# A scan over chunks and a routed expert layer: first decays spread batch by batch, the inverse in two pieces, loads of x in halves

## The chip, the cores and the metric

The kernel runs on one core of a Trainium2 chip. The metric is the device time of one execution in microseconds (us), as the median of several runs. One execution was also taken by the hardware profiler. The engines are TensorE (PE; PEld is its weight load), VectorE (DVE), ScalarE (ACT), GpSimd (POOL) and SyncE (SP), which here issues nearly all loads.

## What is computed

Two parts follow each other. The first is a state-space scan over 768 positions for 4 batches and 8 heads, with head size D = 32 and state size N = 16. The second routes each of the 3072 resulting rows of 256 values to one of 8 experts by cosine similarity, and applies that expert's two matrices.

```python
log_a = np.log(np.clip(a, 1e-06, 1.0))
for c in range(S // 32):                       # the scan, chunk by chunk
    cum = np.cumsum(la, axis=-1)
    L = np.exp(cum[:, :, :, None] - cum[:, :, None, :]) * causal
    M = np.einsum('bhin,bhjn->bhij', Cc, Bc) * L
    y = np.einsum('bhij,bhjd->bhid', M, xc) \
      + np.einsum('bhin,bhnd->bhid', Cc, state) * np.exp(cum)[..., None]
    state = decay_full * state + sum_j(Bc_j xc_j * decay_from_j)
...
xn = x / (norm(x) + 1e-06);  en = expert_emb / (norm(expert_emb) + 1e-06)
logits = xn @ en.T / tau;  e = argmax(logits);  gate = softmax(logits)[e]
out[rows of e] = gate * (np.maximum(x @ w1[e], 0.0) @ w2[e])
```

## The kernel before

The scan goes over six chunks of Q = 128 positions. Each chunk is cut into two pairs of batches, so that there are twelve pairs p = 0..11 and twelve steps s. The order of work is written out by hand: every engine takes its instructions in the order in which the code writes them, and waits on semaphores only where data need it.

Decays are split into factors. `decays` (VectorE) turns the decays `a` of four chunks into running products `f` with one row per chunk, batch and head. `spread_decays` (TensorE, 16 matmuls, batch by batch and within it chunk by chunk) copies each row of `f` to all states of its head, in PSUM tiles `py` (chunks 0 and 1) and `pz` (chunks 2 and 3). `inverse` takes 1/f on VectorE into `r`, `turn_inverse` transposes it on TensorE, and ScalarE copies the outcome to `rT`. `keep_decays` (ScalarE) copies the spread decays of chunks 2 and 3 into `fr`.

For a chunk, `scale_c` makes `cp` = C times the spread decay, and `scale_x` makes `xs` = x times the inverse decay (128x1024, read from `in_x` and `rT`, both in SBUF). For a pair, `scores` multiplies B (`bz`) with `cp` into PSUM tiles `pgA` and `pgB`. `masks` keeps the causal half: VectorE multiplies `pgA` with a mask, while ScalarE copies `pgB` to `g` and GpSimd zeroes the upper half there (`affine_select`, named select below). `outputs` multiplies `g` with `xs` into `py`, `sums` multiplies B (`in_t`) with `xs` for the state, `tokens` turns the pair's outcome into rows.

`bz` has four places of 128x2x512, for chunks modulo 4. Chunks 0 and 1 are filled by ScalarE (`split_b`: two activations of 128x512 with a mask for each half of the states). Chunks 2 and 3, and later 4 and 5 in the places of 0 and 1, come by `load_two` (8 DMAs of 64 KB into the nonzero parts; the rest is cleared ahead by `clear_b` on ScalarE). SP issues the loads in the order of the code, and its DMAs use eight semaphores in turn: the ninth waits until the first has landed.

The start is `begin_scan`: loads, constants, decays, then pairs 0 and 1 up to their masks. `mamba` runs the steps from s = 1. There `outputs(p = s-1)`, at odd steps `sums`, and `tokens(p = s-2)` follow `scores(s)` and `masks(s)`. `norm_embeddings` squares the expert embeddings on ScalarE (`emb_sq`) and takes the root on GpSimd (`emb_r`). `place_consts` writes constants of the router on GpSimd. `fill` are matmuls on zeros that nobody reads. After the scan comes `moe`, 8 experts one after another.

## Time and profile before

| | |
|---|---|
| median of 3 runs | 239.04 us (238.05 to 240.39) |
| the profiled execution: its own time | 239.56 us |
| its span, first to last instruction | 237.8 us |
| TensorE busy, share of the span | 224.9 us, 95% |
| VectorE | 176.8 us, 74% |
| ScalarE | 129.7 us, 55% |
| GpSimd | 99.6 us, 42% |
| moved by DMA | 34.83 MB, mean 146 GB/s |

The scan takes the first 62 us, the experts the rest. Times in the rows below are us from the start of the span. A row of the timeline gives start, duration, engine, line and operation, output tile and input tiles, shape, the count of merged instructions, and in brackets how long the engine was idle before it and who ended that.

### The profile page before, as it was taken

The numbers are of one execution on the slowest core, as the hardware profiler recorded it, in microseconds if no ns is written. First come the engines' busy times: TensorE is split into PE (matmuls) and PEld (weight loads), VectorE is DVE, ScalarE is ACT, GpSimd is POOL, SyncE is SP. The second block draws the span as 40 slices with busy tenths as digits, with TensorE's granted clock in tenths as the row PEclk, the third lists the DMA queues.
The fourth block names the chain that finished last, engine by engine and source line by source line (L and its number), as shares of the span: only waits on it lengthen the run. The fifth ranks groups of instructions, "written<-read, shape, count | busy, mean of one in ns | idle before, by whom it ended". The sixth has DMA issues, their size and how long they took to land. (4 is left out here: it accounts for less than half of the span.)

```text
span 237.8 us, 6603 instructions
## 1 busy us (share of the span) xinstructions
PE 224.9 (95%) x2500; PEld 211.4 (89%) x2500; DVE 176.8 (74%) x467; ACT 129.7 (55%) x349; POOL 99.6 (42%) x125
## 2 busy tenths in 40 slices
PE   7899999999997999999999999999999999999980
PEld 7787878787896999999999999999999999999970
DVE  6896868897775727797768788877887978874850
ACT  6867666663540545652684467358446446637620
POOL 7835321173047507536417234631841623305113
PEclk9999999999999999999999999999999999999997
DMA  5878586475707932626245233824627444201001
GB/s 172 287 215 259 185 231 214 133 211 186 218 3 246 311 121 68 188 76 203 63 158 179 96 132 114 237 61 167 202 68 216 129 140 142 98 3 61 0 3 64
DMA packets 20978, 34.83 MB, mean 146 GB/s; under 512 B 2474, under 2 KB 13968, under 8 KB 20944
## 3 DMA queue, kind: packets, MB, share of 16 engines
q1 hardware_dynamic: 18256, 27.97, 37.5%
q0 software_dynamic: 2592, 6.39, 8.8%
q8 instruction: 20, 0.33, 0.6%
q14 instruction: 14, 0.11, 0.1%
q10 hardware_dynamic: 96, 0.03, 0.1%
HBM read 28.02 MB, written 6.42 MB: 145 GB/s over the span
## 5 line engine op out<-in xcount | busy, mean ns | idle before, releaser
L1141 POOL DMA_INDIRECT out_dram<-yo,to x26 | 29.3, 1128 | 61.5 <-ACT yo L1140 47.3
L1064 DVE TENSOR_TENSOR hT<-bank,hp 128x416 f32<-128x416 f32 (+6 forms) x42 | 22.0, 552 | 14.8 <-ACT hp L1058 9.7
L914 POOL DMA_INDIRECT xg<-rows,table x24 | 27.4, 1143 | 6.7 <-issue 4.5
L1058 ACT COPY hp<-bank 128x416 f32<-128x416 f32 (+6 forms) x42 | 19.9, 475 | 17.7 <-PE bank L1045 17.3
L1070 ACT ACTIVATE hT<-hT 128x416 f32<-128x416 f32 (+6 forms) x42 | 21.6, 524 | 11.3 <-DVE hT L1064 11.2
L628 POOL TENSOR_SCALAR_AFFINE_SELECT g<-g 128x1024 f32<-128x1024 f32 x13 | 17.0, 1315 | 25.6 <-ACT g L627 25.6
L1006 DVE TENSOR_TENSOR ws<-w 128x512 f32<-128x512 f32 x42 | 27.6, 683 | 0.0
L929 POOL TENSOR_TENSOR gr<-gr,half 128x3 f32<-128x3 f32 (+2 forms) x9 | 9.6, 1066 | 31.5 <-ACT sq L925 22.3
L1045 PE MATMUL bank<-ts,w 128*128 128x208 f32 (+6 forms) x112 | 21.8, 328 | 0.0
L1106 PE MATMUL bank<-ts,w 128*128 128x208 f32 (+6 forms) x112 | 21.4, 334 | 0.3 <-ACT yp L1119 0.3
L1045 PE MATMUL bank<-xT,w 128*128 128x208 f32 (+6 forms) x112 | 21.6, 326 | 0.0
L1045 PE MATMUL bank<-ts,ws 128*128 128x208 f32 (+6 forms) x112 | 20.6, 326 | 0.0
L1106 PE MATMUL bank<-hT,w 128*128 128x208 f32 (+6 forms) x112 | 19.5, 326 | 0.0
L1106 PE MATMUL bank<-ts,ws 128*128 128x208 f32 (+6 forms) x112 | 19.5, 326 | 0.0
L1106 PEld LDWEIGHTS bank<-ts,w 128*128 128x128 f32 x112 | 18.1, 190 | 1.3 <-ACT yp L1119 0.6
L1045 PEld LDWEIGHTS bank<-xT,w 128*128 128x128 f32 x112 | 18.8, 190 | 0.0
L1010 DVE TENSOR_TENSOR ts<-hT 128x416 f32<-128x416 f32 (+6 forms) x28 | 15.0, 556 | 5.1 <-ACT hT L1070 4.1
L1045 PEld LDWEIGHTS bank<-ts,ws 128*128 128x128 f32 x112 | 18.5, 190 | 0.1
L1045 PEld LDWEIGHTS bank<-ts,w 128*128 128x128 f32 x112 | 18.0, 190 | 0.5 <-ACT hp L1058 0.4
L1106 PEld LDWEIGHTS bank<-ts,ws 128*128 128x128 f32 x112 | 18.4, 190 | 0.0
L1106 PEld LDWEIGHTS bank<-hT,w 128*128 128x128 f32 x112 | 18.4, 190 | 0.0
L656 PE MATMUL py<-g,xs 128*32 128x128 f32 x384 | 14.1, 276 | 1.5 <-issue 1.1
(255 smaller groups left out, 499.1 us busy)
## 6 DMA issues: line engine op xcount, KB each, us to landing
w<-in_moe_w_dram SPq DMA_DIRECT2D x28, 512.0 KB, 4.3
rows<-yt SPq DMA_DIRECT2D x12, 264.0 KB, 2.3
in_x<-in_x_dram SPq DMA_DIRECT2D x6, 512.0 KB, 4.9
w<-in_moe_w_dram SPq DMA_DIRECT2D x8, 256.0 KB, 3.6
in_c<-in_CT_dram SPq DMA_DIRECT2D x6, 256.0 KB, 3.5
in_t<-in_B_dram SPq DMA_DIRECT2D x6, 256.0 KB, 3.4
bz<-in_BT_dram SPq DMA_DIRECT2D x16, 64.0 KB, 4.3
in_b<-in_BT_dram SPq DMA_DIRECT2D x2, 256.0 KB, 3.3
```

The costliest lines, as they stand in the source:

```text
L628: nc.gpsimd.affine_select(out=g, in_=g, pattern=[[0, 8], [1, Q]], compare_op=ALU.is_ge, fill=0.0, base=0, channel_multiplier=-1)
L656: nc.tensor.matmul(k.py[g : g + 32, v, 128 * i : 128 * i + 128], lhsT=t.xs[:, b + i, 4 * v + q, :], rhs=s.g[:, q, 2 * i + v, :], start=(c ...
L914: s.k.nc.gpsimd.indirect_dma_start(out=s.x[0:p, i, 0:TOK], out_offset=None, in_=rows, in_offset=bass.IndirectOffsetOnAxis(ap=s.at[0:p, i : ...
L929: nc.gpsimd.tensor_tensor(out=s.r[:], in0=s.r[:], in1=k.half[:, 0:nt], op=ALU.pow)
L1006: s.k.nc.vector.tensor_tensor(out=o, in0=in0, in1=in1, op=op)
L1010: s.k.nc.vector.tensor_tensor(out=t[i], in0=in0, in1=in1, op=ALU.subtract)
L1045: k.nc.tensor.matmul(out[:, g], lhsT=lhsT[:, f : f + 128], rhs=rhs, start=(g == 0 and i in (1, 2, 5)), stop=True, skip_group_check=True,)
L1058: nc.scalar.copy(out=u.p[:, {1: 0, 6: 1, 7: 2}[i]], in_=u.a)
L1064: nc.vector.tensor_tensor(out=out, in0=in0, in1=u.p[:, q], op=ALU.add)
L1070: s.k.nc.scalar.activation(c, c, ACT.Relu)
L1106: k.nc.tensor.matmul(out, lhsT=lhsT, rhs=rhs, start=(i in (1, 2) and f == 0), stop=(f == half - 1), skip_group_check=True)
L1141: d = nc.gpsimd.indirect_dma_start(out=k.out[:, :], out_offset=bass.IndirectOffsetOnAxis(ap=s.to[0:p, i : i + 1], axis=0), in_=y[:p], in_o ...
```

## The change

In `begin_scan`:

- `spread_decays` runs in two calls, batches 0 and 1, then 2 and 3. Chunk 0's decays of batches 0 and 1 go to `pgA` in place of `py`, and `scale_c` of these two batches stands between the calls.
- `inverse` of the first four chunks is cut in columns 0..63, ahead of the spread, and 64..127, behind `scale_c`. Its transpose goes to `pz` (in place of `pgB`) behind `scores(0)`, and its copy by ScalarE behind the copy of `masks(0)`. Four matmuls of one column (`spread_last`) bring the last decay of chunk 0 to `py`.
- `masks(0)` stands ahead of `scale_x(0)` on VectorE. Of `scale_x(0)`, batches 0 and 1 stay on VectorE and batches 2 and 3 go to GpSimd, as does the small copy into `cp` (four columns) of chunk 1.
- `norm_embeddings` moves ahead of the spread, thus ahead of `keep_decays` and `masks(0)` on ScalarE, and on GpSimd into the middle of the constants. The last group of constants moves to step 3. The two activations of `split_b` of chunk 1 stand on either side of the copy of `masks(1)`.
- The two clears of `bz` are one of 128x1536 on ScalarE and one of 128x512 on VectorE, both early.

In the loads: x of chunk 0 comes in two DMAs, x of chunks 2 to 5 in two halves, of which (but for chunk 4) the second goes behind `in_t` of the next odd step. B and C of chunk 1 change places. `load_two(4)` moves from step 4 to step 5.

```diff
@@ -69,7 +69,9 @@
     v.memset(k.zero[:], 0.0)
     first = m.tile([128, 1], F32, name="first")
     nc.scalar.activation(first[:], k.zero[:, 0:1], ACT.Square)
-    clear_b(k, 2)
+    k.nc.scalar.copy(
+        out=k.bz[:, 2:4].rearrange("p c v b m -> p (c v b) m")[:, 0 : 3 * NB], in_=bc(k.zero[:, 0:Q], [128, 3 * NB, Q], 1)
+    )
     m_i = m.tile([128, 2], I32, name="m_i")
     v.tensor_single_scalar(m_i[:, 0:1], k.part_i[:], 31, op=ALU.bitwise_and)
     v.tensor_single_scalar(m_i[:, 1:2], k.part_i[:], 16, op=ALU.bitwise_and)
@@ -92,6 +94,7 @@
         out=k.spread[:].rearrange("p b m -> p (b m)"), in0=head_i[:], scalar1=k.m_f[:, 0:1], scalar2=None,
         op0=ALU.is_equal,
     )
+    v.memset(k.bz[:, 3, 1].rearrange("p b m -> p (b m)"), 0.0)
     k.ident = c.tile([128, 128], F32, name="ident")
     g.memset(k.ident[:], 0.0)
     g.affine_select(
@@ -127,6 +130,7 @@
         nc.gpsimd.tensor_copy(out=f[:], in_=i[:])
         return f
 
+    k.xg = [c.tile([128, NT, 2 * Y1], F32, name=f"xg{i}") for i in range(3)]
     k.lows = ramp("lows", 128, BF16)
     k.his = ramp("his", E * NT, pattern=[[32, E], [1, NT]])
     yield
@@ -144,17 +148,13 @@
     k.shift = c.tile([128, E], BF16, name="shift")
     nc.gpsimd.memset(k.shift[:], 0.0)
     nc.gpsimd.memset(k.shift[0:1, 1:E], float(PAD))
+    yield
     k.slots = ramp("slots", E)
     k.step_f = ramp("step", LEFT)
     k.width = c.tile([128, E], F32, name="width")
     for r, w in enumerate(WIDTHS):
         nc.gpsimd.memset(k.width[:, r : r + 1], float(w + PAD if r == 0 else w))
-    k.xg = [c.tile([128, NT, 2 * Y1], F32, name=f"xg{i}") for i in range(3)]
-    yield
-
-
-def clear_b(k, i):
-    k.nc.scalar.copy(out=k.bz[:, i], in_=bc(bc(k.zero[:, 0:Q], [128, NB, Q], 1), [128, 2, NB, Q], 1))
+    yield
 
 
 
@@ -174,8 +174,19 @@
         pool = k.mc if n == "b" else k.inp
         name = f"in_b{c}" if n == "b" else "in_" + n
         v = pool.tile([128, NB, m // NB], F32, name=name, tag=name)
-        k.nc.sync.dma_start(v[:].rearrange("p b m -> p (b m)"), src)
+        h = m // 2 if n == "x" and c == 0 else m
+        for o in range(0, m, h):
+            k.nc.sync.dma_start(v[:].rearrange("p b m -> p (b m)")[:, o : o + h], src[:, o : o + h])
         setattr(t, {"b": "bt", "c": "ct", "x": "x", "t": "b"}[n], v)
+
+
+def load_x(k, c, half):
+
+    t, m = k.ld.setdefault(c, Net()), NB * DM // 2
+    if half == 0:
+        t.x = k.inp.tile([128, NB, DM], F32, name="in_x", tag="in_x")
+    o = m * half
+    k.nc.sync.dma_start(t.x[:].rearrange("p b m -> p (b m)")[:, o : o + m], k.x[c][:, o : o + m])
 
 
 def load_two(k, c):
@@ -223,10 +234,10 @@
         k.nc.sync.dma_start(out, src)
 
 
-def split_b(k, c):
+def split_b(k, c, which=range(2)):
     t = k.ld[c]
     t.bz = k.bz[:, c]
-    for v in range(2):
+    for v in which:
         k.nc.scalar.activation(t.bz[:, v], t.bt[:], ACT.Copy, scale=k.tmask[:, v : v + 1])
 
 
@@ -264,28 +275,45 @@
     yield
 
 
-def inverse(k, kk):
+def inverse(k, kk, cut=slice(0, Q)):
     p = slice(0, 64 if kk else 128)
-    k.nc.vector.reciprocal(out=k.r[p, kk], in_=k.f[p, kk])
-    k.nc.vector.memset(k.r[p, kk, HQ : HQ + 1], 1.0)
-
-
-def turn_inverse(k, kk, ps):
+    k.nc.vector.reciprocal(out=k.r[p, kk, cut], in_=k.f[p, kk, cut])
+    if cut.stop == Q:
+        k.nc.vector.memset(k.r[p, kk, HQ : HQ + 1], 1.0)
+
+
+def turn_inverse(k, kk, ps, keep=True):
     p = 64 if kk else 128
     k.nc.tensor.transpose(ps[:, 0:p], k.r[0:p, kk, :], k.ident[0:p, 0:p])
+    if keep:
+        keep_inverse(k, kk, ps)
+
+
+def keep_inverse(k, kk, ps):
+    p = 64 if kk else 128
     k.nc.scalar.copy(out=k.rT[:, kk, 0:p], in_=ps[:, 0:p])
 
 
 def spread_at(k, c):
+
     return (k.py[:, 0], k.py[:, 1], k.pz[0], k.pz[1], k.py[:, 0], k.py[:, 1])[c]
 
 
-def spread_decays(k, chunks):
+def spread_last(k):
     for b in range(NB):
+        k.nc.tensor.matmul(
+            k.py[:, 0, b : b + 1], lhsT=k.spread[0:32, b, :], rhs=k.f[0:32, 0, Q - 1 : Q], start=True, stop=True,
+            tile_position=(0, 0),
+        )
+
+
+def spread_decays(k, chunks, batches=range(NB)):
+    for b in batches:
         for c in chunks:
             g = 32 * (c % 4)
+            at = k.pgA[:, 0] if c == 0 and b < 2 else spread_at(k, c)
             k.nc.tensor.matmul(
-                spread_at(k, c)[:, 128 * b : 128 * b + 128], lhsT=k.spread[g : g + 32, b, :],
+                at[:, 128 * b : 128 * b + 128], lhsT=k.spread[g : g + 32, b, :],
                 rhs=k.f[g : g + 32, c // 4, :], start=True, stop=True, tile_position=(g, 0),
             )
 
@@ -321,13 +349,13 @@
     k.nc.vector.tensor_tensor(out=t.cp[:, b], in0=t.ct[:, b], in1=f[:, b], op=ALU.mult)
 
 
-def scale_x(k, c, lo=0, n=NB):
+def scale_x(k, c, lo=0, n=NB, vector=True):
     t = k.ld[c]
     if lo == 0:
         t.xs = k.work.tile([128, NB, NH, D], F32, name="xs", tag="xs")
     b = slice(lo, lo + n)
     r = k.rT[:, c // 4, 32 * (c % 4) + 8 * lo : 32 * (c % 4) + 8 * lo + 8 * n]
-    k.nc.vector.tensor_tensor(
+    (k.nc.vector if vector else k.nc.gpsimd).tensor_tensor(
         out=t.xs[:, b].rearrange("p b h d -> p (b h) d"), in0=t.x[:, b].rearrange("p b (h d) -> p (b h) d", h=NH),
         in1=bc(r, [128, 8 * n, D], 2), op=ALU.mult,
     )
@@ -733,43 +761,49 @@
     early_consts(k)
     load(k, 0, "x")
     embeddings(k)
-    load(k, 1, "cb")
+    load(k, 1, "bc")
     load(k, 0, "t")
     fill(k, 9)
     for c in (4, 5):
         load_decays(k, c, nc.sync)
     load(k, 1, "xt")
-    load(k, 2, "cx")
+    load(k, 2, "c")
+    load_x(k, 2, 0)
     first, later, consts = decays(k, 0), decays(k, 1), place_consts(k)
     turn_consts(k)
     next(consts)
-    next(consts)
     next(first)
     next(first)
+    inverse(k, 0, slice(0, HQ))
     split_b(k, 0)
-    clear_b(k, 3)
     load_two(k, 2)
-    spread_decays(k, range(4))
-    inverse(k, 0)
-    scale_c(k, 0, spread_at(k, 0), 0, 2)
-    turn_inverse(k, 0, k.pgB[:, 1, 384:512])
+    norm_embeddings(k)
+    next(consts)
+    spread_decays(k, range(4), (0, 1))
+    scale_c(k, 0, k.pgA[:, 0], 0, 2)
+    spread_decays(k, range(4), (2, 3))
     scale_c(k, 0, spread_at(k, 0), 2, 2)
-    scale_x(k, 0)
-    scores(k, 0)
+    inverse(k, 0, slice(HQ, Q))
     keep_decays(k, 2)
     keep_decays(k, 3)
-    fill(k, 3, k.pz[0][:, 0:Q])
-    nc.scalar.copy(out=k.fr[:, 0, :, Q - 1 : Q], in_=by_batch(spread_at(k, 0))[:, :, Q - 1 : Q])
+    scores(k, 0)
+    turn_inverse(k, 0, k.pz[0][:, 384:512], False)
+    spread_last(k)
+    fill(k, 3, k.pz[1][:, 0:Q])
+    masks(k, 0)
+    keep_inverse(k, 0, k.pz[0][:, 384:512])
+    nc.scalar.copy(out=k.fr[:, 0, :, Q - 1], in_=k.py[:, 0, 0:NB])
     nc.scalar.copy(out=k.fr[:, 1, :, HQ:Q:63], in_=by_batch(spread_at(k, 1))[:, :, HQ:Q:63])
-    norm_embeddings(k)
-    masks(k, 0)
-    split_b(k, 1)
+    scale_x(k, 0, 0, 2)
+    scale_x(k, 0, 2, 2, vector=False)
     scale_c(k, 1, spread_at(k, 1))
     t = k.ld[1]
-    nc.vector.tensor_copy(out=t.cp[:, :, HQ : HQ + 1], in_=t.ct[:, :, HQ : HQ + 1])
+    nc.gpsimd.tensor_copy(out=t.cp[:, :, HQ : HQ + 1], in_=t.ct[:, :, HQ : HQ + 1])
     scores(k, 1)
+    split_b(k, 1, (0,))
     masks(k, 1)
-    k.later = later
+    split_b(k, 1, (1,))
+    k.later, k.consts = later, consts
 
 
 def mamba(k):
@@ -821,11 +855,16 @@
         else:
             even_steps(k, s)
         if s % 2 == 0 and 3 <= s // 2 + 2 < NC:
-            load(k, s // 2 + 2, "cx")
+            load(k, s // 2 + 2, "c")
+            load_x(k, s // 2 + 2, 0)
             if s == 4:
-                load_two(k, 4)
+                load_x(k, 4, 1)
         if s % 2 and 2 <= (s - 1) // 2 + 2 < NC:
             load(k, (s - 1) // 2 + 2, "t")
+            if s == 5:
+                load_two(k, 4)
+            else:
+                load_x(k, (s - 1) // 2 + 2, 1)
         if s >= 8:
             load_weights(k, 0, (2 * s - 16, 2 * s - 15))
         if s in (4, 7, 8):
@@ -868,6 +907,7 @@
     if s == 3:
         next(k.later)
         next(k.later)
+        next(k.consts)
 
 
 def even_steps(k, s):
```

ScalarE's queue in `begin_scan`, from the first fill of `bz` to the copy of `masks(1)`, before (`bz` is B, `fr` the kept decays, `g` the scores, `emb_sq` the squares of the embeddings):

```order
L230 ACTIVATE bz<-in_b_102,tmask 128x512 x2
L157 COPY bz<-zero 128x1024
L276 COPY rT<-pgB 128x128
L294 COPY fr<-pz 128x512 x2
L762 COPY fr<-py 128x4
L763 COPY fr<-py 128x4x2
L363 ACTIVATE emb_sq,emb_r<-emb 8x256
L627 COPY g<-pgB 128x1024
L230 ACTIVATE bz<-in_b_160,tmask 128x512 x2
L627 COPY g<-pgB 128x1024
```

The same stretch of ScalarE's queue in the changed kernel:

```order
L241 ACTIVATE bz<-in_b_102,tmask 128x512 x2
L391 ACTIVATE emb_sq,emb_r<-emb 8x256
L322 COPY fr<-pz 128x512 x2
L655 COPY g<-pgB 128x1024
L294 COPY rT<-pz 128x128
L795 COPY fr<-py 128x4
L796 COPY fr<-py 128x4x2
L241 ACTIVATE bz<-in_b_160,tmask 128x512
L655 COPY g<-pgB 128x1024
L241 ACTIVATE bz<-in_b_160,tmask 128x512
```

The squares stand ahead of the copies of `fr` and `g` now, and the copy of `rT` behind that of `g`.

GpSimd's queue at the place of the constants and of the first select, before:

```order
L127 CAST his<-his_i 128x32
L125 IOTA order_i 128x8
...
L146 MEMSET shift 1x7
L125 IOTA slots_i 128x8
L127 CAST slots<-slots_i 128x8
L125 IOTA step_i 128x32
L127 CAST step<-step_i 128x32
L151 MEMSET width 128x1 x8
L364 TENSOR_TENSOR emb_r<-emb_r,half 8x1
L628 AFFINE_SELECT g<-g 128x1024 x13
```

The same place in the changed kernel:

```order
L130 CAST his<-his_i 128x32
L392 TENSOR_TENSOR emb_r<-emb_r,half 8x1
L128 IOTA order_i 128x8
...
L150 MEMSET shift 1x7
L656 AFFINE_SELECT g<-g 128x1024
L358 TENSOR_TENSOR xs<-in_x,rT 128x512
L801 COPY cp<-in_c 128x4
L656 AFFINE_SELECT g<-g 128x1024 x4
```

The root of the embeddings' squares now stands ahead of eleven small constants (of which "..." leaves out nine), and half of x and the copy into `cp` stand between the first two selects.

TensorE's queue from the end of the spread to the first scores of pair 1, before ("..." leaves out the rest of the scores of pair 0):

```order
L287 MATMUL py<-f,spread 128x128 x2
L287 MATMUL pz<-f,spread 128x128 x2
L275 MATMUL pgB<-ident,r 128x128
L611 MATMUL pgA<-cp,bz 128x128 x2
...
L611 MATMUL pgB<-cp,bz 128x128 x2
L239 MATMUL pz<-zero 128x128 x3
L611 MATMUL pgA<-cp,bz 128x128 x2
```

The same place in the changed kernel:

```order
L315 MATMUL py<-f,spread 128x128 x2
L315 MATMUL pz<-f,spread 128x128 x2
L639 MATMUL pgA<-cp,bz 128x128 x2
...
L639 MATMUL pgB<-cp,bz 128x128 x2
L287 MATMUL pz<-ident,r 128x128
L304 MATMUL py<-f,spread 128x1 x4
L250 MATMUL pz<-zero 128x128 x3
L639 MATMUL pgA<-cp,bz 128x128 x2
```

The transpose of the inverse has moved from ahead of the scores of pair 0 to behind them, and with the four matmuls of one column it stands ahead of the same three matmuls on zeros.

## Rows read from the trace of the kernel before

**Rows 1.** Busy time of the engines from 12 to 22 us: the stretch, its length, busy time and instructions of PE, PEld, DVE, ACT and POOL, then the granted clock of TensorE as a share of full speed, the DMA share and GB/s.

```profile
12.00:22.00 10.00, 9.85 (x287) 8.34 (x279) 7.47 (x18) 6.68 (x13) 5.19 (x4) 1.00 0.79 218
```

**Rows 2.** Timeline of TensorE, 6 to 15 us: the spread (L287), scores (L611), matmuls on zeros (L239), outputs (L656), and the turn of the embeddings (L377).

```profile
6.17 0.42 PE L287 MATMUL py<-f,spread 32*128 32x128 f32 x2
...
6.83 0.27 PE L287 MATMUL py<-f,spread 32*128 32x128 f32 x2
...
7.72 0.38 PE L611 MATMUL pgA<-cp,bz 32*128 32x128 f32 x2 [0.35 <-ACT rT L276]
...
8.83 0.94 PE L239 MATMUL pz<-zero 128*128 128x128 f32 x6
10.27 0.38 PE L611 MATMUL pgA<-cp,bz 32*128 32x128 f32 x2 [0.51 <-DVE g L625]
...
11.37 1.09 PE L656 MATMUL py<-g,xs 128*32 128x128 f32 x32
...
12.85 0.38 PE L611 MATMUL pgA<-cp,bz 32*128 32x128 f32 x2
...
14.53 0.29 PE L377 MATMUL pz<-ident,emb 8*128 8x8 f32 x2
```

**Rows 3.** Timeline of VectorE, 3 to 13 us: first decays (L250), inverse (L269), `scale_c` (L321), `scale_x` (L330), masks (L625), the small copy into `cp` (L769).

```profile
3.35 0.23 DVE L250 TENSOR_SCALAR aw<-a 128x126 f32<-128x126 f32 x1 [0.88 <-DMA a<-in_a_dram]
...
5.20 0.95 DVE L269 RECIPROCAL r<-f 128x128 f32<-128x128 f32 x1
...
7.16 0.75 DVE L321 TENSOR_TENSOR cp<-in_c,py 128x256 f32<-128x256 f32 x2 [0.88 <-PE pz L287]
7.83 1.22 DVE L330 TENSOR_TENSOR xs<-in_x,rT 128x1024 f32<-128x1024 f32 x1
8.99 1.22 DVE L625 TENSOR_TENSOR g<-pgA,mask 128x1024 f32<-128x1024 f32 x1
10.13 0.68 DVE L321 TENSOR_TENSOR cp<-in_c,py 128x512 f32<-128x512 f32 x1
10.84 0.53 DVE L769 COPY cp<-in_c 128x4 f32<-128x4 f32 x1
11.48 1.23 DVE L625 TENSOR_TENSOR g<-pgA,mask 128x1024 f32<-128x1024 f32 x1
```

**Rows 4.** Timeline of ScalarE, 3 to 10 us: a clear of `bz` (L157), `split_b` (L230), `rT`, `fr`, the squares of the embeddings (L363), the copy of `masks(0)` (L627).

```profile
3.12 1.03 ACT L157 COPY bz<-zero 128x1024 f32<-128x1024 f32 x1
4.51 1.33 ACT L230 ACTIVATE bz<-in_b,tmask 128x512 f32<-128x512 f32 x2 [0.37 <-DMA in_b<-in_BT_dram]
...
7.41 0.27 ACT L276 COPY rT<-pgB 128x128 f32<-128x128 f32 x1 [0.63 <-PE pgB L275]
7.57 1.08 ACT L294 COPY fr<-pz 128x512 f32<-128x512 f32 x2
...
8.63 0.41 ACT L363 ACTIVATE emb_sq<-emb 8x256 f32<-8x256 f32 x1
...
9.04 0.98 ACT L627 COPY g<-pgB 128x1024 f32<-128x1024 f32 x1
```

**Rows 5.** The landing of the early loads: SP's wait for `in_x` ahead of its next issue of decays (us in total, times, longest), that issue in SP's timeline, and the DMA packets in the stretches 5.75 to 6.00 and 7.00 to 7.25 us.

```profile
SPq L166 <- DMA in_x<-in_x_dram: 1.6, 1, 1.6
...
7.52 0.80 SPq L166 DMA_DIRECT2D a<-in_a_dram  x2
...
DMA packets 51, 0.07 MB, mean 264 GB/s; under 512 B 30, under 2 KB 32, under 8 KB 51
...
DMA packets 88, 0.10 MB, mean 406 GB/s; under 512 B 38, under 2 KB 40, under 8 KB 88
```

**Rows 6.** Timeline of GpSimd, 6 to 11 us: first and last of the eleven constants that the change leaves ahead of the first select, the root (L364), the first select (L628).

```profile
6.14 0.13 POOL L125 IOTA order_i<- 128x8 int32 x1
...
7.60 0.10 POOL L146 MEMSET shift<- 1x7 bf16 x1
...
9.70 0.58 POOL L364 TENSOR_TENSOR emb_r<-emb_r,half 8x1 f32<-8x1 f32 x1
10.26 1.09 POOL L628 TENSOR_SCALAR_AFFINE_SELECT g<-g 128x1024 f32<-128x1024 f32 x1
```

**Rows 7.** The same two operations at the same time in a later step: `scale_x` in VectorE's timeline and a select in GpSimd's.

```profile
37.79 2.15 DVE L330 TENSOR_TENSOR xs<-in_x,rT 128x1024 f32<-128x1024 f32 x1
...
37.77 1.09 POOL L628 TENSOR_SCALAR_AFFINE_SELECT g<-g 128x1024 f32<-128x1024 f32 x1 [3.29 <-ACT g L627]
```

**Rows 8.** The later loads: SP's issue of `in_t` of chunk 2, time from issue to landing of `in_t` (count, size, median), VectorE's first step behind `scale_x(2)`, SP's issue of B of chunks 4 and 5, ScalarE's copy of rows at step 5, time to landing of `bz`, and the scores of pair 8 on TensorE, which read B of chunk 4.

```profile
17.43 0.88 SPq L177 DMA_DIRECT2D in_t<-in_B_dram  x1
...
in_t<-in_B_dram SPq DMA_DIRECT2D x6, 256.0 KB, 3.4
...
22.02 0.42 DVE L689 TENSOR_TENSOR V<-T,pz 128x256 f32<-128x256 f32 x1 [2.06 <-ACT yt L716]
...
28.08 4.43 SPq L186 DMA_DIRECT2D bz<-in_BT_dram  x8
...
30.20 0.66 ACT L716 COPY yt<-pz 128x264 f32<-128x264 f32 x2 [0.89 <-PE pz L705]
...
DMA to landing us min/median/max: 2.3/4.3/7.0
...
39.65 0.38 PE L611 MATMUL pgA<-cp,bz 32*128 32x128 f32 x2
```

## Prediction

> **What bounds the kernel now.** I read the busy shares by stretch first. From 12 us on TensorE is busy for 9.85 of 10 us at a granted clock of 1.00, the full 2.4 GHz, while VectorE has 7.47 and ScalarE 6.68 [rows 1]. What this change can give or take is therefore the time at which TensorE's dense stretch begins. I take the first scores of pair 2 as the mark, at 12.85 us [rows 2]: all behind it follows TensorE's order, so a shift of this mark should arrive at the end nearly whole.
>
> Then I read the five queues side by side up to that mark, to see which wait ends last. The second pass of the spread of batch 1 starts at 6.17, the last pass at 6.83 [rows 2], and VectorE's `scale_c` starts at 7.16, behind all of it [rows 3]. Scores of pair 0 start at 7.72, released by the copy of `rT` on ScalarE [rows 2]. VectorE then makes `xs` (7.83) and only at 8.99 the mask, which releases scores of pair 1 at 10.27. `outputs(0)` starts at 11.37, right behind the select on GpSimd, which ran from 10.26 to 11.35 [rows 2, 6]. Scores of pair 2 wait for the second mask on VectorE, 11.48 to 12.71 [rows 3].
>
> **The change part by part.** *Spread by batch and the inverse behind it.* Half of the spread is through at 6.17 + 0.42 = 6.59. `scale_c` follows at 6.64 (the gap is 0.05 us before: 7.10 to 7.16) and takes about 0.4 (0.75 for two). Scores no longer wait for `rT` and start at about 7.1 in place of 7.72: 0.6 us won. They take until the mask can start: 8.99 less 7.72 bounds it at 1.27, so scores end near 8.3. On VectorE the second `scale_c` and the second half of the inverse (0.95 / 2 = 0.5, [rows 3]) fit in between, 7.1 to 8.15. The mask runs 8.33 to 9.55, in place of 8.99 to 10.21: 0.65 won. The clear of 128x512 on VectorE lies in the 0.88 us in which VectorE waits for the decays [rows 3]: nothing, unless it takes more than that. ScalarE's clear grows from 1.03 to about 1.5 us, so that `split_b` starts at about 4.65 in place of 4.51 [rows 4] and ends at 6.0, a microsecond ahead of the scores: nothing.
>
> *The squares of the embeddings ahead of `keep_decays` and the mask's copy.* This is where I expect the gain to go. ScalarE is free at 6.0, and its next instruction now waits for the embeddings. Their load stands behind x in SP's queue. SP's issue at 7.52 had waited 1.6 us for x, so x landed near 7.5; the small packets that only the embeddings and landings make come in two bursts, 30 under 512 B at 5.75 to 6.00 and 38 at 7.00 to 7.25 [rows 5]. In the kernel before the squares ran at 8.63 and saw nothing of this. I take 7.5 for the landing, with 6.0 and 8.0 as bounds. Then squares 7.5 to 7.9, `fr` to 8.95 (two copies, 1.08), the copy of `masks(0)` 8.85 to 9.85 (0.98) [rows 4]. It ends 0.15 ahead of before (10.02), not 0.65. `rT` follows, 9.75 to 10.05 (0.27).
>
> *TensorE's queue.* The transpose goes to `pz` and so waits until `fr` is copied, 8.95. Behind it stand four matmuls of one column and the three on zeros, ahead of scores of pair 1. The six zero passes take 0.94 - 0.14 = 0.8 us up to the next start. For the four small matmuls of two passes each the nearest row is the turn of the embeddings, two passes in 0.21 up to the next start [rows 2]: 0.4 to 0.85, I take 0.6. Scores of pair 1 can start at 9.0 + 0.1 + 0.6 + 0.8 = 10.5 in place of 10.27. The zeros, which lay in a wait before, lie on the path now.
>
> *GpSimd.* The root waits for the squares: 8.0 to 8.6 (0.58). Behind it stand the eleven constants, 6.14 to 7.70 before, 1.56 us: GpSimd is free at 10.2, 0.35 behind the copy that the select needs [rows 6].
>
> *Half of x on VectorE against the select.* `xs` (two inputs in SBUF) is ready when `rT` is, at about 10.1; the select on GpSimd at about 10.2. At 37.77 us the two met: the select took its 1.09, and `xs` 2.15 in place of 1.22 [rows 7]. So one stands until the other is through. With VectorE first, as these two times have it, `xs` of 128x512 runs 10.1 to 10.7 (half of 1.22), and the select 10.75 to 11.85: 0.5 us later than before. The Trainium skill has this as a rule (SBUF — State Buffer, section Who interferes with whom): a VectorE instruction with two SBUF inputs contends with a GpSimd instruction that reads SBUF, and whichever is issued first holds the port for its whole length. The rows agree, and the rule speaks against this edit, which puts such a VectorE instruction next to the select and a second reader behind it; by it the order of the two is decided by a tenth of a microsecond, hence the second case below.
>
> *Half of x on GpSimd.* No row shows a multiply of that size there. At the select's rate per element 512 elements take 0.55 us; with two inputs at twice the select's whole price it is 2.2. I take 1.1, a whole select's. (By the Trainium skill, GPSIMD Engine Reference, section Performance versus the Vector engine, an add of two inputs costs about 2.6 cycles per element, an estimate of 1.1 us for 512; no run here shows it, and the sum would be the same.) It runs 11.85 to 12.95, and the copy into `cp`, 0.53 on VectorE before with a wait inside [rows 3], follows until 13.1.
>
> **The sum.** `outputs(0)` starts at 11.9 in place of 11.37, behind the select, and lasts 0.9 up to the next start. `sums` needs all of `xs`, 12.95, and ends at 13.3. The mask of pair 1 follows its scores (10.5 + 1.2 = 11.7) and ends at 12.95, the split of B's second half behind the copy of that mask at 13.35. So scores of pair 2 start at about 13.3 in place of 12.85: 0.45 us later. VectorE has shed 0.6 + 0.53 us, but nobody waits for that any more. On the profiled execution's 239.56 this gives 240.0; that execution lies 0.5 above the median of the runs, so 239.04 + 0.45 = 239.5; since a part may be taken back in later waits I say **239.4 us**.
>
> *The later loads.* The second half of x of chunk 2 goes out behind `in_t`, issued at 17.43, so at some 17 to 18.3, and lands about 3.4 later, near 21. `scale_x(2)` (1.22) then ends near 22; VectorE had 2.06 us of idle time ahead of its next step at 22.02 [rows 8]. Nothing, with little to spare. B of chunks 4 and 5 was issued from 28.08 to 32.5. Now it goes behind the rows of step 5 (ready at 30.86) and `in_t`: 31.9 to 36.3. Pair 8 reads it at 39.65. With a landing time of about 4 us it is just hidden; the 16 such loads took 2.3 to 7.0, median 4.3 [rows 8]. I take nothing, and the rest as a rival.
>
> **The rivals.** *The gain arrives (faster).* If the embeddings land by 6.0, as the first burst of packets would have it, the squares are through before the spread. `fr` ends at 8.2, scores of pair 1 start at 8.25 + 1.5 = 9.8, the mask's copy ends at 9.3 and the select at 10.4; if VectorE's `xs` costs no wait there, `outputs(0)` follows at 11.0, and scores of pair 2 at about 12.5: 0.35 us earlier, 238.7. Against it speaks the second burst, at 7.0 to 7.25.
>
> *GpSimd takes the port first.* If the select starts at 9.9, `xs` on VectorE waits until 11.0, `scale_c(1)` goes to 12.3, the mask of pair 1 ends at 13.45, and scores of pair 2 start at 13.5: 0.65 later, 239.7.
>
> *The head isn't felt.* Later waits of TensorE, such as for gathered rows, could end when they ended before: 239.0. Against it speaks that what they wait for hangs on TensorE's own rows.
>
> *B of chunk 4 comes late (slower).* One DMA landing decides scores of pair 8. The last of the eight is issued at about 35.9; from a landing time of 4.2 us on (39.65 + 0.45 - 35.9) TensorE stands still, at 7.0, the longest seen, for 2.8 us. At 5.5 it is 1.3 us: 239.4 + 1.3 = 240.7. For it speaks the median of 4.3, against it that the bounds leave half of these loads shorter, and that the last of the eight must be among the long ones.
>
> **How the numbers follow.** Chances: forecast 0.40, gain arrives 0.24, port the other way 0.14, not felt 0.10, B late 0.12. A multiply of 2.2 us on GpSimd would move `sums` to 14.4 and the time to 240.5. The runs before spread from 1.0 below to 1.35 above their median. From 238.7 less 0.9 to 240.7: the range is 237.8 to 240.7. What a measurement of this kernel can tell from no change is about 1%, 2.4 us. Only a late B with a long landing passes that on the slow side (0.05); no case does on the fast side, and I leave 0.03 for what I have not seen. Within 1%: 0.92.
>
> **What would show it.** In the profile of the changed kernel: scores of pair 0 near 7.1 and the first mask near 8.3 (the spread); ScalarE idle from 6.0 to about 7.5 ahead of the squares, ended by the embeddings' DMA; scores of pair 1 not before 10; the first select ending behind 11.5, next to a `scale_x` on VectorE; scores of pair 2 at 13.1 to 13.5. Scores of pair 8 must not wait for `bz`. I am wrong if the squares run by 6.5, if select and `xs` don't touch, or if the mark moves by half a microsecond and the end does not.

## The result, and the profile after

The changed kernel takes 240.61 us (median of 20 runs, 239.23 to 242.04), the kernel before 239.03 (20 runs, 237.6 to 242.95): a ratio of 1.0071, 95% interval 1.0051 to 1.009. It is slower by 1.6 us; 0.4 was forecast, and the time lies inside the range. The mark of the prediction, the first scores of pair 2, came at 14.61 in place of 12.85 [rows 2].

From the timeline of the changed kernel, all engines (scores are L639 now, `outputs` L684, the turn L287, `spread_last` L304, zeros L250, `sums` L702, squares L391, `fr` L322, `rT` L294, `xs` L358, `cp` L349, masks L653 and L655, select L656):

```profile
6.81 0.38 PE L639 MATMUL pgA<-cp,bz 32*128 32x128 f32 x2
...
7.79 0.41 ACT L391 ACTIVATE emb_sq<-emb 8x256 f32<-8x256 f32 x1 [1.84 <-DMA emb<-in_moe_expert_emb_dram]
...
8.07 1.22 DVE L653 TENSOR_TENSOR g<-pgA,mask 128x1024 f32<-128x1024 f32 x1 [0.36 <-PE pgB L639]
...
8.20 1.03 ACT L322 COPY fr<-pz 128x512 f32<-128x512 f32 x2
...
9.14 1.00 ACT L655 COPY g<-pgB 128x1024 f32<-128x1024 f32 x1
...
9.34 0.30 PE L287 MATMUL pz<-ident,r 128*128 128x128 f32 x1 [1.35 <-DVE g L653]
...
9.56 1.05 PE L304 MATMUL py<-f,spread 32*128 32x1 f32 x8
...
10.45 1.09 POOL L656 TENSOR_SCALAR_AFFINE_SELECT g<-g 128x1024 f32<-128x1024 f32 x1
...
10.54 0.94 PE L250 MATMUL pz<-zero 128*128 128x128 f32 x6
...
11.41 0.38 PE L639 MATMUL pgA<-cp,bz 32*128 32x128 f32 x2
...
11.51 0.27 ACT L294 COPY rT<-pz 128x128 f32<-128x128 f32 x1 [1.37 <-PE pz L250]
...
11.81 0.69 DVE L358 TENSOR_TENSOR xs<-in_x,rT 128x512 f32<-128x512 f32 x1 [2.51 <-ACT rT L294]
...
11.86 1.55 POOL L358 TENSOR_TENSOR xs<-in_x,rT 128x512 f32<-128x512 f32 x1 [0.32 <-ACT rT L294]
...
12.42 0.68 DVE L349 TENSOR_TENSOR cp<-in_c,py 128x512 f32<-128x512 f32 x1
...
13.15 1.08 PE L684 MATMUL py<-g,xs 128*32 128x128 f32 x32 [0.57 <-DVE cp L349]
...
14.05 0.63 PE L702 MATMUL pz<-xs,in_t 128*32 128x64 f32 x32
...
14.61 0.38 PE L639 MATMUL pgA<-cp,bz 32*128 32x128 f32 x2
```

The first scores gained 0.9 us (6.81, 7.72 before), and from there everything slips. ScalarE stands still for 1.84 us until the embeddings land; the copies to `fr` and with them the turn come behind that. The turn, the eight small passes and the zeros take TensorE from 9.34 to 11.41. `rT` is copied only behind the zeros, `xs` behind `rT`, `cp` of chunk 1 behind `xs`, and the first outputs behind that `cp`, since they write `py`, which it reads.

The table puts all runs side by side: the start of the first scores and of pair 2's in each profiled execution (two or three where there were as many), and the ratio of the timed runs to the kernel before on the same chip. The profiled execution of the head alone is a slow one (243.21 us, the median of its runs 240.4), so its 18.00 is not set beside the other marks.

| kernel | scores 0 | scores, pair 2 | ratio, 95% |
|---|---|---|---|
| before | 7.72, 7.12, 7.12 | 12.85, 12.75, 12.57 | 1 |
| changed | 6.81, 6.54 | 14.61, 15.58 | 1.0071, 1.0051 to 1.009 |
| loads alone (e3) | 7.00 | 12.39 | 1.0007, 0.9983 to 1.0031 |
| head alone (e5) | 6.55 | 18.00 | 1.0087, 1.0058 to 1.0116 |
| squares back (e1) | 6.55 | 13.32 | 1.0029, 0.9998 to 1.006 |
| no zeros (e2) | 6.87 | 13.31 | 1.0052, 1.0023 to 1.0082 |
| both (e6) | 7.24 | 13.73 | 1.0036, 1.001 to 1.0062 |
| both, old loads (e7) | 7.19 | 13.65 | 1.0042, 1.0009 to 1.0076 |
| x on VectorE (e4) | 6.56 | 15.86 | 1.009, 1.0055 to 1.0125 |
| wait filled (e12) | 6.77 | 14.49 | 1.0097, 1.0064 to 1.0129 |
| x first (e9) | 6.86, 6.64 | 13.09, 13.98 | 1.0067, 1.0037 to 1.0097 |
| x first, zeros (e13) | 7.19 | 13.69 | 1.0032, 1.0000 to 1.0063 |
| halves round the mask (e10) | 7.11, 7.30 | 12.38, 12.57 | 1.0028, 0.9992 to 1.0064 |

### The profile page after: what moved, and what is told of

The parts are those of the page before. It is cut to its first block, busy times and chain, and to the rows that moved or that the text cites. A ratio compares the mean times of both kernels' runs of the same rounds, so it can differ in the third digit from the quotient of the medians.

```text
span 238.6 us, 6626 instructions
## 1 busy us (share of the span) xinstructions
PE 225.0 (94%) x2508; PEld 211.8 (89%) x2508; DVE 178.4 (75%) x468; ACT 129.1 (54%) x348; POOL 99.8 (42%) x127
## 5 line engine op out<-in xcount | busy, mean ns | idle before, releaser
L1181 POOL DMA_INDIRECT out_dram<-yo,to x26 | 28.3, 1090 | 60.7 <-ACT yo L1180 46.5
L954 POOL DMA_INDIRECT xg<-rows,table x24 | 27.9, 1162 | 6.7 <-issue 4.5
L656 POOL TENSOR_SCALAR_AFFINE_SELECT g<-g 128x1024 f32<-128x1024 f32 x13 | 16.8, 1295 | 22.5 <-ACT g L655 22.5
L1050 DVE TENSOR_TENSOR ts<-hT,ts 128x416 f32<-128x416 f32 (+6 forms) x28 | 14.9, 551 | 0.2
```

The source lines that it names most:

```text
L656: nc.gpsimd.affine_select(out=g, in_=g, pattern=[[0, 8], [1, Q]], compare_op=ALU.is_ge, fill=0.0, base=0, channel_multiplier=-1)
L954: s.k.nc.gpsimd.indirect_dma_start(out=s.x[0:p, i, 0:TOK], out_offset=None, in_=rows, in_offset=bass.IndirectOffsetOnAxis(ap=s.at[0:p, i : ...
L1050: s.k.nc.vector.tensor_tensor(out=t[i], in0=in0, in1=in1, op=ALU.subtract)
L1181: d = nc.gpsimd.indirect_dma_start(out=k.out[:, :], out_offset=bass.IndirectOffsetOnAxis(ap=s.to[0:p, i : i + 1], axis=0), in_=y[:p], in_o ...
```

## The experiments

### Head or loads

> The kernel before, with the changed loads alone: x of the chunks in halves, B ahead of C for chunk 1, and B of chunk 4 a step later. Theory A (head): the first scores of pair 2 stay at 12.85, the time is that of the kernel before within 0.3, 239.0. Theory C (loads): the head stays and the time is 240.2 to 240.8, with a wait for a transfer between 17 and 45 us.

The edit is the load part of the diff ahead of the prediction, on the kernel before:

```diff
-    load(k, 1, "cb")
+    load(k, 1, "bc")
...
-    load(k, 2, "cx")
+    load(k, 2, "c")
+    load_x(k, 2, 0)
```

> The changed kernel with all loads as in the kernel before; so the other half of the loads-alone run. Theory A (the head costs all of it): the first scores of pair 2 at 14.6, the time that of the changed kernel, 1.6 above the kernel before. Theory D (the loads cost something of their own, since the second half of x of chunk 2 is issued at 17 to 18 us instead of 9.8 and lands at 21 to 22; the late head hides most of that): the scaled x of chunk 2 starts without a wait, and the time is 0.2 to 0.5 below the changed kernel. Theory C (loads alone): the time of the kernel before.

```diff
-    load(k, 1, "bc")
+    load(k, 1, "cb")
...
-    load(k, 2, "c")
-    load_x(k, 2, 0)
+    load(k, 2, "cx")
```

The loads alone cost nothing that can be measured (the interval reaches to 0.3%), and the head alone costs what the whole change costs. Theory C falls. The second half of x of chunk 2 does land late, as theory D has it (timelines of VectorE and TensorE in the run with the loads alone; its scores are L622, its mask L636):

```profile
21.13 1.23 DVE L341 TENSOR_TENSOR xs<-in_x,rT 128x1024 f32<-128x1024 f32 x1 [2.76 <-DMA in_x<-in_x_dram]
...
26.03 0.38 PE L622 MATMUL pgA<-cp,bz 32*128 32x128 f32 x2 [1.31 <-DVE g L636]
```

The scores of pair 5 waited 1.3 us in that execution for a mask that stands behind this step in VectorE's queue, but the median doesn't show it, nor do the two other pairs that differ by loads alone (changed and head alone; both and both with old loads). So theory D's price is not confirmed in the times. Its wait is in the profiles all the same, and it comes back below.

### What holds the head

> The changed kernel, with the squares of the embeddings put back behind ScalarE's two copies to fr, so that they no longer stand ahead of these. Theory A (the loss is in the head, and the first cause is that ScalarE waits at the squares until the embeddings land at 7.8 us): the copies to fr run at 6.8 to 7.8 instead of 8.2 to 9.2, TensorE's turn of the inverse comes at 8.1 instead of 9.34, the second scores at about 10.2 instead of 11.41, the first scores of pair 2 at 13.3 instead of 14.61, and the time is 1.2 below the changed kernel, about 239.4. Theory B (the turn waits for VectorE's first mask product, which ends at 9.29, and not for fr): the turn stays at 9.34 and the time at 240.6. Theory C (the loss is in the later loads, and the head's slip is made up by step 9, as the two profiled executions read): the head is 1.2 earlier and the time stays at 240.6.

```diff
     load_two(k, 2)
-    norm_embeddings(k)
     next(consts)
...
+    norm_embeddings(k)
     masks(k, 0)
```

> The changed kernel without the three products of zeros between the first and the second scores; they compute nothing. Theory A (their 0.9 us stand on the path, before the second scores and before the copy to rT, which waits for the whole tile pz): rT is copied right behind ScalarE's mask copy, at 10.2 instead of 11.51, the second scores come at 10.55 instead of 11.41, the first outputs at 11.9 instead of 13.15, the first scores of pair 2 at 13.4 instead of 14.61, and the time is 1.2 below the changed kernel, about 239.4. Theory B (the head is led by VectorE or GpSimd, and the zeros fill a wait): rT moves, the scores of pair 2 stay within 0.3 of 14.6, and the time stays at 240.6. Theory C (the later loads cost the time): head earlier, time 240.6. A fourth possibility: without the zeros TensorE's granted clock falls between 10 and 12 us, and the second scores take over 1.3 us instead of 0.9.

```diff
     spread_last(k)
-    fill(k, 3, k.pz[1][:, 0:Q])
     masks(k, 0)
```

> The changed kernel with both undone at once: the squares behind the copies to fr, and no products of zeros. The second scores then wait for ScalarE's mask copy, at 9.5 us; GpSimd's half of x ends at about 12.2 and the sums follow it, so the first scores of pair 2 come at 12.85 (13.3 with either alone). Theory A (only the head counts): 0.4 less than either alone, 0.2 to 0.4 above the kernel before. Theory D (x of chunk 2 lands at 21 to 22 and holds the scores of pair 5 at 26.0 to 26.9, however early the head is): the time is that of the run with the squares back, 0.6 to 0.7 above the kernel before.

> The same kernel with the loads of the kernel before. Theory D: x of chunk 2 is scaled at 18.2 to 18.5 without a wait, the scores of pair 5 come at 24.3 to 25.0 instead of 26.0 to 26.9, and the time is 0.6 to 1.0 below the kernel with both undone and the changed loads, at or up to 0.4 below the kernel before. Theory A: the same as that kernel within 0.3. If the gain at pair 5 is given back at a later transfer, the two kernels' scores stand level again by pair 8.

These two are the two edits above at once, the second with the loads of before. From the timelines of the run with the squares back, and of the one without the zeros:

```profile
6.50 1.07 ACT L322 COPY fr<-pz 128x512 f32<-128x512 f32 x2 [0.51 <-PE pz L315]
...
7.67 0.30 PE L287 MATMUL pz<-ident,r 128*128 128x128 f32 x1
...
8.10 0.42 ACT L391 ACTIVATE emb_sq<-emb 8x256 f32<-8x256 f32 x1 [0.52 <-DMA emb<-in_moe_expert_emb_dram]
```

```profile
9.88 0.25 ACT L294 COPY rT<-pz 128x128 f32<-128x128 f32 x1
...
10.16 0.69 DVE L358 TENSOR_TENSOR xs<-in_x,rT 128x512 f32<-128x512 f32 x1 [0.81 <-ACT rT L294]
...
10.29 1.52 POOL L656 TENSOR_SCALAR_AFFINE_SELECT g<-g 128x1024 f32<-128x1024 f32 x1
```

One call holds the squares and the root, so the first edit also moves the root on GpSimd, behind the constants. With the squares back `fr` is copied at 6.50 and the turn comes at 7.67, ahead of the end of VectorE's mask: theory B falls (the profile had named that mask as the releaser at 9.34). Without the zeros `rT` is copied at 9.88, right behind ScalarE's mask copy. Each moves the mark by 1.3 us, as theory A had it. In time 1.2 us, 0.5%, was expected of each; the squares gave 0.4% back, the zeros 0.2%. The intervals of these two overlap, and both reach into that of the changed kernel, so neither gain in time is clear of the noise.

Two things that the profiles and the runs show stand against these gains. One is the late x of chunk 2, here without the zeros:

```profile
21.11 1.63 DVE L358 TENSOR_TENSOR xs<-in_x,rT 128x1024 f32<-128x1024 f32 x1 [1.82 <-DMA in_x<-in_x_dram]
...
26.67 0.38 PE L639 MATMUL pgA<-cp,bz 32*128 32x128 f32 x2 [1.14 <-DVE g L653]
```

TensorE stood still for 1.14 us ahead of the scores of pair 5, and for 1.06 with the squares back. In these two executions the scores of pair 8 came at 40.51 and 40.76, behind the 40.21 of the changed kernel, although the mark had been 1.3 ahead. The other is the clock: eight of the twelve runs without the zeros have a mean granted clock below 0.990, and none of those with the squares back. That is the fourth possibility of the expectation; the profiled execution, at 1.00 through the head, doesn't show it.

Both together should have come to 12.85 and came to 13.7, with no better ratio. Two things stood against it. The passes of the spread were 0.21 us apart in these two executions (in the second for its first half), as in the first profile of before, not 0.11, so that the first scores came 0.3 to 0.7 us later. And `xs` met the select (both with old loads):

```profile
9.91 1.10 POOL L654 TENSOR_SCALAR_AFFINE_SELECT g<-g 128x1024 f32<-128x1024 f32 x1 [0.30 <-ACT g L653]
...
10.02 1.52 DVE L356 TENSOR_TENSOR xs<-in_x,rT 128x512 f32<-128x512 f32 x1 [0.34 <-ACT rT L292]
```

Here the select came first and `xs` took 1.52; without the zeros `xs` came first (10.16) and the select took 1.52 in place of 1.09. This is the rule of the Trainium skill that the prediction cites (SBUF — State Buffer, section Who interferes with whom), in both orders. The first of the two runs also shows what the copy of `rT` does not wait for: the small passes write `py` and run until 10.01.

```profile
8.96 1.05 PE L304 MATMUL py<-f,spread 32*128 32x1 f32 x8
...
9.82 0.25 ACT L294 COPY rT<-pz 128x128 f32<-128x128 f32 x1
```

> The changed kernel with all of the first chunk's scaled x on VectorE, nothing of it on GpSimd. Theory A with VectorE in the chain (xs, then the scaled C of chunk 1, then the first outputs and the second mask product): VectorE's step grows from 0.69 to 1.3, the first outputs come at 13.75 instead of 13.15, the first scores of pair 2 at 15.2 instead of 14.61, the time is 0.6 above the changed kernel, 241.2. Rival (GpSimd's half, done at 13.41, is what the sums wait for, and holds VectorE at the shared port): the scores of pair 2 stay or come earlier, the time is 240.6 or less.

```diff
-    scale_x(k, 0, 0, 2)
-    scale_x(k, 0, 2, 2, vector=False)
+    scale_x(k, 0)
```

VectorE's step grew from 0.69 to 1.22, but the mark of 15.86 can't be set beside 14.61, because the granted clock fell in this execution. Beside the second profile of the changed kernel, where it fell as well (15.58), it is 0.3 later. The times don't tell the two apart: the half on GpSimd is worth little either way.

### The granted clock

> The changed kernel once more, for a second profiled execution. The squares start when the embeddings land; if that varies as in the other runs (7.6 to 8.7 us), TensorE's wait ahead of the turn is 1.1 to 2.5 us, and where it is over 1.8 us the granted clock falls to 0.5 to 0.6 between 11 and 15 us, as in the runs with x on VectorE and with the head alone; the first scores of pair 2 then come at 15.8 to 18 instead of 14.6.

> The changed kernel with five more products of zeros (1.45 us) on TensorE between the first scores and the turn, into a part of py that nothing uses, where it waits for ScalarE. Theory G (part of the loss is the granted clock, which falls in those executions in which TensorE idles longest there): the turn comes at 9.35 to 9.5 as before, the granted clock stays at 1.00 to 15 us, and the time is 0.3 to 0.7 below the changed kernel, with fewer executions of a low mean clock. Theory A alone (only the waits count): the time of the changed kernel, 240.6, or 0.1 above.

```diff
     scores(k, 0)
+    fill(k, 5, k.py[:, 0, 0:Q])
     turn_inverse(k, 0, k.pz[0][:, 384:512], False)
```

TensorE's wait ahead of the turn in the second profile of the changed kernel, and in the head alone:

```profile
9.41 0.30 PE L287 MATMUL pz<-ident,r 128*128 128x128 f32 x1 [1.70 <-ACT fr L322]
...
10.23 0.30 PE L285 MATMUL pz<-ident,r 128*128 128x128 f32 x1 [2.51 <-ACT fr L320]
```

Stretches of the same two, with the columns of [rows 1]:

```profile
9.00:11.00 2.00, 1.59 (x12) 1.49 (x13) 0.03 (x1) 1.21 (x2) 1.68 (x12) 1.00 0.90 288
11.00:13.00 2.00, 2.00 (x29) 1.78 (x32) 0.96 (x2) 1.02 (x4) 1.52 (x2) 0.56 0.89 298
13.00:15.00 2.00, 2.00 (x48) 1.71 (x45) 1.55 (x2) 1.18 (x2) 0.87 (x3) 0.58 0.97 288
```

```profile
8.00:10.00 2.00, 0.00 (x0) 0.00 (x0) 1.04 (x1) 1.32 (x4) 0.69 (x2) 1.00 0.45 164
10.00:12.00 2.00, 1.77 (x10) 1.66 (x10) 0.00 (x0) 1.04 (x2) 1.72 (x10) 0.73 0.82 307
12.00:14.00 2.00, 2.00 (x14) 1.78 (x18) 0.17 (x1) 0.47 (x4) 0.55 (x2) 0.50 0.88 267
```

TensorE waited 1.70 (the expectation had named 1.8) and 2.51 us, and then ran at about half, 1.2 GHz, for some microseconds; the first outputs took 1.54 and 1.94 in place of 1.08. In the first profile of the changed kernel it waited 1.35 and kept 2.4 GHz. How long it waits hangs on the embeddings, which landed between 7.6 and 8.7. Of the 20 timed runs of the changed kernel 10 have a mean clock of 0.987 or less (median 240.98) and 10 one of 0.989 or more (240.24); the kernel before keeps 0.990 or more in each of the 29 runs beside e1 to e4. In the five other kernels with at least four runs on either side of 0.990 (head alone, no zeros, both, both with old loads, x first) those below it have the longer median too, by 0.2 to 2.0 us. The mean is a rough sign: the clock is 0.50 in the last microseconds of every profiled execution as well, and a mean of 0.989 stands beside 1.00 through the head in one of them (x first, zeros) and beside a fall in another (x first again). With the wait filled all ten runs keep 0.990 or more, as theory G had it, but the time did not fall. So the clock scatters single executions, and a gain in the median from keeping it is not shown for this kernel.

> The kernel with both undone and the loads of before (its run: first scores of pair 2 at 13.65, time 1.0 above the kernel before), with two further steps put back: ScalarE copies rT right behind the turn, ahead of the squares and of its mask copy, and VectorE's half of x comes ahead of its first mask product instead of behind it. Theory E (what is left of the loss is x behind the mask: rT stands behind ScalarE's mask copy and the half of x then meets GpSimd's select, 1.52 instead of 0.69 us, with the scaled C of chunk 1 and the first outputs behind it): x at 8.3 to 9.0, mask to 10.2, scaled C to 10.9, first outputs at 11.0 instead of 12.2, the first scores of pair 2 at 12.7, and the time within 0.3 of the kernel before. Rival F (what is left is the turn and the eight small products on TensorE, which stay): outputs at 12.2, the time stays 1.0 above the kernel before.

The two further steps, against the kernel with both undone and the old loads:

```diff
-    turn_inverse(k, 0, k.pz[0][:, 384:512], False)
+    turn_inverse(k, 0, k.pz[0][:, 384:512])
     spread_last(k)
     norm_embeddings(k)
+    scale_x(k, 0, 0, 2)
     masks(k, 0)
-    keep_inverse(k, 0, k.pz[0][:, 384:512])
...
-    scale_x(k, 0, 0, 2)
     scale_x(k, 0, 2, 2, vector=False)
```

> The kernel with x ahead of the mask once more. Theory G: where the mean clock is under 0.990, the granted clock has fallen somewhere between 9 and 15 us, behind TensorE's wait for the mask (1.2 us in the first profile), and the first scores of pair 2 come at 13.8 to 15 instead of 13.1. Theory H: clock 1.00 there, and the pause at the third block, 0.29 in the first profile, is longer.

> The kernel with x ahead of the mask, with three products of zeros (0.87 us) put back on TensorE behind the eight small ones, but into a part of py that ScalarE's copy to rT does not wait for; TensorE waits there for the mask in any case. Theory G (that kernel's time, 1.5 above the kernel before although its profiled head is only 0.34 late, comes from executions in which the granted clock fell: their mean clock is 0.982 to 0.989): the mean clock is 0.990 or more in nearly all executions, and the time is 0.3 to 0.8 above the kernel before. Theory H (it comes from TensorE's pauses at its instruction blocks, which this does not change): the time stays 1.3 to 1.6 above.

Against the kernel with x first:

```diff
     spread_last(k)
+    fill(k, 3, k.py[:, 0, Q : 2 * Q])
     norm_embeddings(k)
```

With x first the mark fell to 13.09 (12.7 expected) and the time did not follow: 1.6 us above the kernel before, where 0.3 was expected. Seven of the eleven runs have a mean clock below 0.990. The second profile shows one such execution (granted clock in the column behind GpSimd's):

```profile
11.00:13.00 2.00, 2.00 (x55) 1.88 (x52) 1.23 (x1) 1.45 (x2) 1.49 (x3) 0.65 0.99 309
13.00:15.00 2.00, 2.00 (x54) 1.83 (x49) 0.84 (x4) 0.77 (x2) 0.73 (x1) 0.50 1.04 362
```

and the mark at 13.98. With zeros that nobody waits for, the ratio is 1.0032 and eleven of twelve runs have a mean clock of 0.990 or more, as theory G expected; the two intervals overlap. So zeros ahead of the second scores do hold the clock. In the changed kernel they cost their place, 0.87 us of TensorE ahead of the second scores, and their tile: with these scores at 11.41 the first outputs could have started at 12.51 (1.10 behind, as in the kernel before, 10.27 and 11.37), and they started at 13.15.

### Halves round the mask, and TensorE's pauses

> A kernel made from what the runs showed: the decays spread by batch as in the changed kernel, but the inverse in one piece and turned ahead of the first scores (into a part of py that nothing else uses), the last decays of batches 0 and 1 copied from pgA before the scores overwrite it (so no eight small products), x of chunk 0 loaded in halves, its first half scaled ahead of VectorE's mask product and its second behind the scaled C of chunk 1, the squares behind the mask copy, all on VectorE; loads otherwise as before. If the parts add up as their traces say, the first outputs come at 10.3 to 10.8 (11.24 before), the first scores of pair 2 at 11.9 to 12.3 (12.75 in the second profiled execution of before), and the time is 0.4 to 0.8 below the kernel before. If the half of x meets GpSimd's select and takes 1.2 to 1.5 us, the second mask product comes no earlier than before and the time is the same within 0.3.

The core of its edit, on the changed kernel with the loads of before but x of chunk 0 in halves:

```diff
+    inverse(k, 0)
...
+    turn_inverse(k, 0, k.py[:, 0, 0:128])
     scale_c(k, 0, spread_at(k, 0), 2, 2)
+    scores(k, 0)
...
-    spread_last(k)
+    scale_x(k, 0, 0, 2)
     masks(k, 0)
...
+    norm_embeddings(k)
     scale_c(k, 1, spread_at(k, 1))
+    scale_x(k, 0, 2, 2)
```

> The kernel with x in halves round the mask once more. Theory H (in its first profiled execution TensorE paused for 1.53 us at 24.4, as the third 16 KB block of queue q8 ended 2.5 us behind the start of the scores of pair 4; the pause differs by execution): the first scores of pair 2 again at 12.3 to 12.5; the pause is there only if that block ends over 1.1 us behind the scores of pair 4, and without it the span is 1.5 shorter, 236.0.

> The kernel before once more, for a second profiled execution. If TensorE's pauses of half a microsecond that the profile calls issue (at 18, 23.5 and 42.5 us in the first profiled execution) belong to the kernel, they stand at the same places, and the first scores of pair 2 come at 12.85 again. If they and the slow first products differ from execution to execution, they stand elsewhere, and the first scores of pair 2 come at 12.4, as in the run with the loads alone, whose head is this kernel's.

> The kernel before a third time. Theory H: a pause of TensorE in the outputs at 22 to 25 us if the third block of q8 ends over 1.1 us behind the start of the scores of pair 4 (1.6 behind in the first profile: 0.55; 0.7 behind in the second: none). The first scores of pair 2 at 12.75 to 12.85, and the span 235.6 plus the pauses.

The mark came at 12.38 and 12.57, up to 0.5 ahead of before, and the gain of 0.4 to 0.8 us did not come: no version here beats the kernel before. The first profile of the halves shows a pause of TensorE that nothing in the trace ends; the DMA view of 22 to 23 us shows a packet of queue q8 ahead of it:

```profile
24.41 0.64 PE L684 MATMUL py<-g,xs 128*32 128x128 f32 x15 [1.53 <-issue]
```

```profile
q8 instruction: 1, 0.02, 5.8%
```

Queue q8 moves instructions in single packets of 16 KB, in the first 50 us one every 3.5 to 7.4 us. I took the end of the third one against the start of pair 4's scores in all 18 profiled executions. It ended 1.1 to 1.6 us behind them in six executions, which have pauses of 0.29 to 0.56 between 22.6 and 24.6 us (the first of before, 1.6 behind: 0.55); 2.5 behind in this one (22.0 to 22.95, scores at 20.45), with the longest pause; and at most 0.8 behind in the other eleven, which have none there. The second and third profiles of before are among these (0.7 and 0.8), with spans of 235.6 and 235.9 in place of 237.8. The repeat of this kernel had the block 1.5 behind, paused for 0.56, and once more for 0.79 at 42.75. Of the eleven executions in which the scores of pair 4 start before 21.7 seven have the pause, of the seven in which they start later none; so an earlier head seems to meet its own instructions more often. The second block fits: only in the first profile of before did it end over 1.0 behind the scores of pair 3 (1.5), and only there do the scores of pair 4 come 4.73 behind those of pair 3, in place of 4.3. That the late block causes the pause is an inference from 18 executions; I did not move a block, and what delays it is open.

## Why the prediction was wrong

The direction was right, and so were both of the reasons named for the loss, the squares and TensorE's queue: taking either away moves the mark. The size of the loss was wrong. The step that failed is the copy of `rT`, whose wait for the zeros the sum put at nothing.

- *"`rT` follows, 9.75 to 10.05"*: it came at 11.51. I had the transpose in `pz` waiting for `fr`, but not its copy waiting for the zeros, which go to another part of the same tile. The run without zeros shows that this was the wait. That the copy did not wait for the small passes, which write `py`, shows that the tile counts. It is the largest miss of a single term.
- *"`outputs(0)` starts at 11.9 in place of 11.37, behind the select"*: 13.15, behind `cp` of chunk 1. With the mask put first, `xs` and that `cp` stand between `rT` and the outputs on VectorE; I followed `xs` only as far as the select. Of the 1.25 us that were missed here, 0.6 is this wait (13.15 less the 12.51 from above), and the other 0.6 TensorE's queue, by the next two terms in the main.
- *"I take 0.6"* for the four small matmuls: 0.98 up to the next start, beyond the bound of 0.85. The row taken for it had eight columns in two passes; one column is no cheaper.
- *"I take 7.5 for the landing"*: 7.79, and 8.68 in one run, which is beyond the bound of 8.0. Together with the small matmuls this makes most of the way from 10.5 to 11.41 for the second scores.
- *The select behind `xs`*, 10.75 to 11.85: it ran from 10.45 to 11.54, ahead of `xs` at 11.81, since `rT` was late. That the two do not touch was one of the prediction's own signs of being wrong. They met when the zeros were gone or the squares were back.
- *"Scores of pair 2 wait for the second mask on VectorE"*: in the rows TensorE has no idle time there. `outputs`, `sums` and these scores follow each other at 11.37, 12.27 and 12.85 before, and at 13.15, 14.05 and 14.61 in the changed kernel. So the mark hangs on the first outputs.
- *A multiply of 1.1 on GpSimd*: 1.55 beside VectorE's half, 1.05 where no such half ran (x first). The term held; the share on top fits the port, since it came only beside that half.
- *The later loads at nothing*: right in the time. Scores of pair 8 came at 40.21 without a wait for B, so that rival did not occur. x of chunk 2 landed near 21, as forecast, which is just in time for a head as late as this one; with the earlier heads above TensorE waited 1.1 to 1.3 us ahead of pair 5.
- *"a shift of this mark should arrive at the end nearly whole"*: it passes through the scan where nothing else waits. Against the second profile of before the changed kernel has its first scores of pairs 2, 5 and 8 later by 1.86, 1.86 and 1.87. It does not hold for an earlier mark, as the scores of pair 8 above show. From the mark to the end of the span the 18 executions take 222.4 to 225.6 us, a spread of twice the loss, so that one span tells little about a mark.
- *The time from the profile*: the profiled execution of before carried pauses of 0.55 and 0.52 and a slow spread, none of which belong to the kernel. So the gain of 0.6 expected for the spread was measured against an execution that was late itself: the first scores come at 7.12 in two other profiles, and the gain is 0.3 to 0.6.

What is left of the loss when squares and zeros are back, 0.3 to 0.4%, I can place only in part: `xs` behind the mask next to the select, the turn and the small passes, and the clock each showed in a profile, but no run takes one of them away with a ratio clear of the others. A hint lies in the clock: with both undone and the old loads, the eight runs with a mean clock of 0.990 or more have a median of 238.1, the kernel before 238.2, and the four below it 240.1.

## What to carry to other kernels

Where an instruction is moved up in a queue, look at what it waits for that its old place had hidden: the squares were free at 8.63 and held three engines when moved to 6.0. Where filler shares a PSUM tile with something that is copied out, the copy waits for the filler. A load that is moved later into a wait holds up a version of the kernel in which that wait is gone. And a profile of a kernel that is tuned to half a microsecond is one draw: take a second one before a gain of that size is read from it.
